# A second step's products moved into two accumulator banks, and the last accumulators copied in halves

## The chip, the cores and the metric

The kernel runs on one core of one Trainium2 chip. TensorE (PE) multiplies, VectorE (DVE) and ScalarE (ACT) do the elementwise work, SyncE (SP) issues most of the loads. The metric is the time of one execution on the device, in microseconds; the kernel before takes 663.96 (median of three runs, 663.55 to 664.05).

## The reference

Two small attentions exchange between 512 tokens and 32 states of each of 8 batches and 8 heads, and a two-layer network runs over the concatenated rows (8 x 544 = 4352 rows):

```python
scores = (x @ state.T) / 8;   a  = softmax(scores);   xread = a @ state      # 512 rows a batch
scores2 = (state @ x.T) / 8;  a2 = softmax(scores2);  sread = a2 @ x         # 32 rows a batch
y = concat(xread, sread)                    # (8 batches, 544 rows, 512 = heads x 64)
h = y @ w_in                                # 512 -> 2048
g = where(h >= 1, h, where(h <= -1, 0, (h + 1)**2 / 4))
out = g @ w_out                             # 2048 -> 512, all in float32
```

## The kernel before

`xread` is never formed: `state @ w_in` is computed instead ("states times W_in", `sw_product`, L410), and the attention's weights (`ath`, `atl`) are multiplied by it. Every float32 factor is split into a high and a low part of a shorter type, and a product is three matmuls: high by high, high by low, low by high (L477 to L479, L534 to L536).

A batch `b` goes through eight steps `j`; a step makes 256 of the 2048 hidden columns. In a step, `sw` of the step is made (sixteen small matmuls into the one `mm` tile, two banks), copied out as `swh` by ACT and `swl` by DVE; the *first products* (`Hidden.product`, L461) give two tiles of 128 hidden columns by 512 tokens, each from two halves `q` of the contraction and three matmuls a half, so twelve matmuls; ACT and DVE turn them into `g` (`relu`, `square`, `bound`, `high`, `low`, L481 to L502); and the *output products* (`g2`, L515) multiply `gh` and `gl` by the step's part of W_out into four accumulators of 128 tokens by 512, one bank each, with twenty-four matmuls that `g2` can issue in two halves. The four accumulators of a batch stay over its eight steps, and `store` (L542) copies them out in the last. The ninth "batch" is the 256 state rows of all batches together, with two accumulators and four steps; its `store` copies the first with ACT and the second with DVE, each followed by four DMAs of 32 rows.

PSUM has eight banks: two in the `mm` tile, two for the first products (`ps_h`, tag `h`), four with the tag `acc`. Ahead of the first output product the `acc` banks hold the score tiles of batch 0 (two) and `warmed`, into which filler matmuls go (`warm`, L195).

Batch 0 is special. Its weights are still on their way and have to be decoded: each chunk of W_in or W_out is loaded raw, ACT makes a high part (L588), ACT or DVE a low part (L580, L575), DVE joins them (L596), and for W_out ACT and DVE split the result (L603, L607). The order of this part is written by a planner (`Plan`, L23). Each operation is declared with an engine, a cost in microseconds, what it comes after, and which shared tile it takes. On PE and SP the order is that of the declarations; on ACT and DVE the planner simulates: whenever an engine is idle it starts the ready operation with the longest tail of costs behind it. Between the first scores and the first output product it puts fillers where it expects PE to idle (L125). After batch 0 the code is written in plain order (L807).

In that plan PE's declared order at the start is: scores, `sw0`, first half (`q` = 0) and second half of step 0's products, `sw1`, the transposes `e2p` of the second attention, step 1's products, `sw2`, first half of step 0's output products, `sr` (the second attention's read), second half, step 2's products, `sw3`, and so on (L776 to L789). A step's products take the two `h` banks once the `bound`s of the step before are through, and its buffer `u` once `gl` of the step before is.

Of the kernel before, what the change touches and what calls it, by code (L numbers as in the profile page):

```python
# [8 lines left out]
F32 = mybir.dt.float32  # L9
# [13 lines left out]
class Plan:  # L23
# [13 lines left out]
    def op(self, key, engine, cost, run, after=(), take=(), ends=()):  # L37

        after = list(after)
        prior = self.last.get(engine) if engine in ("PE", "SP") else None  # L40
        self.last[engine] = key
        self.ops[key] = [engine, cost, run, after, list(take), list(ends), prior]
# [95 lines left out]
def state_exchange_moe(  # L138
# [17 lines left out]
    nc = tc.nc  # L156
    B, P, NT, H, D = x.shape
    S = NT * P
    NS = 32
    DM = H * D  # L160
    NPR = H // 2
    CI = 256
    NC = w_in.shape[0]
# [3 lines left out]
    TOK = S + NS  # L167
# [5 lines left out]
    work = ctx.enter_context(tc.tile_pool(name="work", bufs=2))  # L173
# [4 lines left out]
    def ps_acc(name):  # L178
        return ps.tile([P, DM], F32, tag="acc", bufs=4, name=name)

    def ps_h(name):
        return ps.tile([P, 512], F32, tag="h", bufs=2, name=name)
# [6 lines left out]
    half = small.tile([P, 1], F32, name="half")  # L189
# [35 lines left out]
    class Attention:  # L225


        def __init__(self, b):
            self.b = b
            self.xt = loaded.pop(("xt", b))  # L230
            self.ath = work.tile([P, 2, S], F32R, tag="ath", name=f"ath{b}")
            self.atl = work.tile([P, 2, S], F32R, tag="atl", name=f"atl{b}")
            att_of[b] = (self.ath, self.atl)
# [196 lines left out]
    def sw_high(b, c):  # L430
        pt, wh, _ = sw_of[b, c]
        nc.scalar.copy(out=wh, in_=pt)

    def sw_low(b, c):
        pt, wh, wl = sw_of[b, c]
        nc.vector.tensor_tensor(out=wl, in0=pt, in1=wh.bitcast(F32), op=ALU.subtract)
# [14 lines left out]
    acc = {}  # L451

    class Hidden:


        def __init__(self, b, j):
            self.b, self.j = b, j
            self.u = work.tile([P, 2, S], F32, tag="u", bufs=1, name=f"u{b}_{j}")
            self.hs = []

        def product(self, i, ks=None):  # L461
            b, j = self.b, self.j
            n = n_of[b]
            per = S // n
            ah, al = att_of[b]
            nk = ah.shape[1]
            if not ks or 0 in ks:
                self.hs.append(ps_h(f"h{b}_{j}_{i}"))
            hp = self.hs[i]
            for r in range(per):  # L470
                f = (2 * j + i) * per + r
                wh, wl = chunk[b, f // 2]
                sl = slice((f % 2) * P, (f % 2 + 1) * P)
                o = hp[:, r * n:(r + 1) * n]
                for k in ks or range(nk):
                    first, last = k == 0, k == nk - 1
                    nc.tensor.matmul(o, lhsT=wh[:, k, sl], rhs=ah[:, k], start=first, stop=False)  # L477
                    nc.tensor.matmul(o, lhsT=wl[:, k, sl], rhs=ah[:, k], start=False, stop=False)  # L478
                    nc.tensor.matmul(o, lhsT=wh[:, k, sl], rhs=al[:, k], start=False, stop=last)  # L479
# [35 lines left out]
    def g2(b, j, half=None):  # L515
        n = n_of[b]
        per = S // n
        nt = n // P
        if b not in acc:
            acc[b] = [ps_acc(f"acc{b}_{t}") for t in range(nt)]  # L520
        gh, gl = gs[b, j]
        last = j == NJ // per - 1
        pairs = [(i, t) for i in range(2 * per) for t in range(nt)]
        if last:
            pairs.sort(key=lambda p: p[1])
        if half is not None:
            pairs = pairs[half * len(pairs) // 2:][:len(pairs) // 2]
        for i, t in pairs:
            f = 2 * per * j + i
            oh, ol = wo[f // 2][:, 0, f % 2], wo[f // 2][:, 1, f % 2]  # L530
            c0 = (i % per) * n + t * P
            lh, ll = (v[:, i // per, c0:c0 + P] for v in (gh, gl))
            a = acc[b][t]
            nc.tensor.matmul(a, lhsT=lh, rhs=oh, start=f == 0, stop=False)  # L534
            nc.tensor.matmul(a, lhsT=lh, rhs=ol, start=False, stop=False)  # L535
            nc.tensor.matmul(a, lhsT=ll, rhs=oh, start=False, stop=f == NF - 1)  # L536
            if last and i == 2 * per - 1:
                store(b, t)
# [3 lines left out]
    def store(b, t):  # L542
        if t == 0:
            outs[b] = rawp.tile([P, NT, DM], F32, tag="raw", name=f"o{b}")
        o = outs[b][:, t]
        if b == B and t % 2:
            nc.vector.tensor_copy(o, acc[b][t])
        else:
            nc.scalar.copy(out=o, in_=acc[b][t])  # L549
        if b < B:  # L550
            r0 = b * TOK + t * P
            nc.scalar.dma_start(out=out[r0:r0 + P, :], in_=o)
        else:
            for i in range(4):
                r0 = (4 * t + i) * TOK + S
                (nc.sync if i % 2 else nc.scalar).dma_start(
                    out=out[r0:r0 + NS, :], in_=o[i * NS:(i + 1) * NS]
                )

# [127 lines left out]
    def hidden_ops(b, j):  # L689
        k = (b, j)  # L690
        for i in range(2):
            op(("relu", i) + k, "ACT", 0.58, lambda i=i: hid[k].relu(i), [("p", i) + k], ends=[("h", i) + k],
               take=[("u", ("u",) + k)] if i == 0 else [])
        op(("square",) + k, "ACT", 0.97, lambda: hid[k].square(), [("relu", 0) + k, ("relu", 1) + k])
        for i in range(2):
            op(("bound", i) + k, "DVE", 0.6, lambda i=i: hid[k].bound(i), [("square",) + k], ends=[("h", i) + k])
        op(("gh",) + k, "ACT", 0.97, lambda: hid[k].high(), [("bound", 0) + k, ("bound", 1) + k],
           ends=[("u",) + k], take=[("g", ("g",) + k)])
        op(("gl",) + k, "DVE", 1.14, lambda: hid[k].low(), [("gh",) + k], ends=[("u",) + k])

    def tensor(key, cost, f, after=(), take=(), ends=()):
        op(key, "PE", cost, f, after, take, ends)
# [6 lines left out]
    def sw_ops(b, c, n):  # L709
        tensor(("sw", b, c), 0.35 + 0.35 * n, lambda: sw_product(b, c, n), [("w", c + i) for i in range(n)],  # L710
               take=[("mm", ("sw", b, c)), ("w", ("wc", b, c))])
        op(("swh", b, c), "ACT", 0.5 * n, lambda: sw_high(b, c), [("sw", b, c)], ends=[("sw", b, c)])
        op(("swl", b, c), "DVE", 0.6 * n, lambda: sw_low(b, c), [("swh", b, c)], ends=[("sw", b, c)])

    def g1_ops(b, j):
        if j == 0:
            for q in range(2):
                for i in range(2):
                    need = [(x, b, j) for x in ("swh", "swl")] + [(x, b, q) for x in ("ath", "atl")]
                    tensor(("p", i, b, j) if q else ("p0", i), 0.72, lambda i=i, q=q: product(i, b, j, [q]), need,  # L720
                           take=[] if q else [("h", ("h", i, b, j))], ends=[("wc", b, j)])
            return
        for i in range(2):
            need = [(x, b, j) for x in ("swh", "swl")] + [(x, b, q) for x in ("ath", "atl") for q in range(2)]
            tensor(("p", i, b, j), 1.4, lambda i=i: product(i, b, j), need, take=[("h", ("h", i, b, j))],
                   ends=[("wc", b, j)])

    def g2_ops(b, j, half):
        k = (b, j)
        tensor(("g2", half) + k, 2.75, lambda: g2(b, j, half), [("gh",) + k, ("gl",) + k, ("wol", j), ("sc done", 0)],  # L730
               ends=[("g",) + k])


# [21 lines left out]
    for side in range(2):  # L755
        tensor(("sc", 0, side), 0.6, lambda side=side: att_start(0, side), [("dma", "xt", 0, side)],
               ends=[("xt", 0)])
# [6 lines left out]
                          take=[("mm", ("e2p", 0))]),  # L764
        1: lambda: tensor(("sr", 0), 1.1, lambda: atts[0].read2(), [("kept", 0), ("dma", "xn", 0)],
                          take=[("mm", ("sr", 0))], ends=[("e2", 0), ("xn", 0)]),
        2: lambda: tensor(("sc", 1), 1.1, lambda: att_start(1), [("dma", "sb", 1), ("dma", "xt", 1)],
                          take=[("mm", ("sc", 1))], ends=[("xt", 1)]),
        3: lambda: tensor(("rt", 0), 0.3, lambda: atts[0].keep2(), [("rs", 0)], take=[("mm", ("rt", 0))]),
        4: lambda: tensor(("e2p", 1), 0.9, lambda: atts[1].turn2(), [("exp2", 1, 0), ("exp2", 1, 1)],  # L770
                          take=[("mm", ("e2p", 1))]),
        5: lambda: tensor(("sr", 1), 1.1, lambda: atts[1].read2(), [("kept", 1), ("dma", "xn", 1)],
                          take=[("mm", ("sr", 1))], ends=[("e2", 1), ("xn", 1)]),
        6: lambda: tensor(("rt", 1), 0.3, lambda: atts[1].keep2(), [("rs", 1)], take=[("mm", ("rt", 1))]),
    }
    for j in range(NJ):  # L776
        g1_ops(0, j)
        hidden_ops(0, j)
        if j + 1 < NC:
            sw_ops(0, j + 1, 1)  # L780
        if j:
            g2_ops(0, j - 1, 0)
        if j in between:
            between[j]()
        if j == 2:
            att_ops1(1)
            att_ops2(1)
        if j:
            g2_ops(0, j - 1, 1)  # L789
    sw_ops(1, 0, 2)  # L790
    import os
    with guard:
        plan.emit(warm, ("sc", 0, 0), ("g2", 0, 0, 0))

# [74 lines left out]
```

## Time and profile before

| | |
|---|---|
| median of three runs | 663.96 us (663.55 to 664.05) |
| the profiled execution's own time | 664.0 us |
| its span | 662.2 us |
| PE busy | 653.9 us (99%), 4442 matmuls |
| DVE busy | 340.3 us (51%) |
| ACT busy | 356.5 us (54%) |
| granted TensorE clock | 1.00 |
| HBM traffic | 34.08 MB read, 8.91 MB written |

The profile comes from one execution. A row of its timeline gives the start, the length, the engine, the line of the kernel and the tile written and read; "x12" merges neighbours. What stands in brackets is how long the engine was idle before the row and what ended that. Rows of one engine overlap by some 0.05 to 0.1 us, so that the distance of two starts is the better measure of an operation that runs back to back. A matmul's record (0.39 us) is longer than its distance from the next (0.23 us), because matmuls are pipelined.

### The profile page before, as it was taken

To read this page: it belongs to the slowest core of one execution; us is meant where nothing else is said; L and a number is where in the kernel's file an instruction comes from. 1 tells how busy PE (TensorE), PEld (TensorE's weight loads), DVE (VectorE), ACT (ScalarE), POOL (GpSimd) and SP (SyncE) were. 2 spreads that over 40 slices of the span, in tenths; PEclk is the share of its full clock that TensorE was granted. 3 is DMA by queue.
4 is the path that set the end of the run, shared out by engine and by line. 5 is a ranking of instruction groups with operands and counts; after the bars stand their busy time and mean duration, and the time that the engine had idled before them with its cause. 6 is when DMAs were issued, how large, how long until landed. Compare 5 with 4: busy or idle time off the path is not lost.

```text
span 662.2 us, 10304 instructions
## 1 busy us (share of the span) xinstructions
PE 653.9 (99%) x4442; PEld 514.2 (78%) x4442; DVE 340.3 (51%) x490; ACT 356.5 (54%) x462; POOL 0.8 (0%) x7
## 2 busy tenths in 40 slices
PE   8999999999999999999999999999999999999997
PEld 6677777777787777777787777777778777778896
DVE  5999947623673239433563338433563343333431
ACT  4899847544554446544554447444653454454642
POOL 0000000000000000000000000000000000000000
PEclk9999999999999999999999999999999999999999
DMA  8986103010301003010301002010100000000101
GB/s 359 400 359 249 64 10 119 0 65 0 120 10 64 1 4 124 0 65 0 128 1 64 1 24 105 0 65 0 65 1 1 1 33 32 1 1 1 63 1 33
DMA packets 11085, 43.65 MB, mean 66 GB/s; under 512 B 1312, under 2 KB 1440, under 8 KB 7968
## 3 DMA queue, kind: packets, MB, share of 16 engines
q1 hardware_dynamic: 6096, 34.28, 13.6%
q10 hardware_dynamic: 4944, 8.72, 3.5%
q8 instruction: 35, 0.57, 0.3%
q14 instruction: 10, 0.08, 0.0%
HBM read 34.08 MB, written 8.91 MB: 65 GB/s over the span
## 4 chain that ended last, share of the span: by engine, by line
PE 91%; ACT 5%; DVE 3%; issue 0%; DMA 0%; POOL 0%; SPq 0%; ACTq 0%; POOLq 0%
PE acc L534 19%; PE acc L536 18%; PE acc L535 18%; PE h L477 9%; PE h L479 9%; PE h L478 9%; PE sw L417 5%; PE sc L253 1%; PE sr L350 1%; PE e2p L333 1%; PE warmed L198 1%; ACT u L482 1%; ACT u L485 1%; ACT raw_i L588 1%; DVE w L596 1%; ACT wo L603 0%
## 5 line engine op out<-in xcount | busy, mean ns | idle before, releaser
L534 PE MATMUL acc<-wo,gh 128*128 128x512 f32 x544 | 218.8, 402 | 0.0
L535 PE MATMUL acc<-wo,gh 128*128 128x512 f32 x544 | 212.3, 390 | 0.0
L536 PE MATMUL acc<-wo,gl 128*128 128x512 f32 x544 | 212.2, 390 | 0.0
L482 ACT ACTIVATE u<-h,half 128x512 f32<-128x512 f32 x136 | 93.7, 693 | 219.9 <-PE h L479 202.6
L488 DVE SCALAR_TENSOR_TENSOR u<-u,h 128x512 f32<-128x512 f32 x136 | 87.0, 680 | 206.7 <-ACT u L485 206.7
L534 PEld LDWEIGHTS acc<-wo,gh 128*128 128x128 f32 x544 | 102.1, 188 | 40.1 <-ACT u L482 12.8
L536 PEld LDWEIGHTS acc<-wo,gl 128*128 128x128 f32 x544 | 102.1, 188 | 22.5 <-issue 0.4
L535 PEld LDWEIGHTS acc<-wo,gh 128*128 128x128 f32 x544 | 102.2, 188 | 19.4 <-DVE wo L607 0.3
L502 DVE TENSOR_TENSOR gl<-u,gh 128x1024 fp32r<-128x1024 f32 x68 | 83.2, 1224 | 33.0 <-ACT gh L497 32.0
L497 ACT CAST gh<-u 128x1024 fp32r<-128x1024 f32 x68 | 71.8, 1056 | 50.3 <-DVE u L488 49.9
L485 ACT ACTIVATE u<-u 128x1024 f32<-128x1024 f32 x68 | 72.5, 1065 | 1.3
L417 PE MATMUL sw<-w,sb 64*32 64x256 f32 x1024 | 36.0, 383 | 1.8 <-DVE w L596 1.3
L417 PEld LDWEIGHTS sw<-w,sb 64*32 64x32 f32 x1024 | 15.1, 106 | 17.9 <-issue 8.8
L479 PE MATMUL h<-atl,sw_0h 128*128 128x512 f32 x60 | 23.6, 393 | 0.3 <-DVE atl L306 0.2
L477 PE MATMUL h<-ath,sw_0h 128*128 128x512 f32 x60 | 23.5, 394 | 0.0
L549 ACT COPY o<-acc 128x512 f32<-128x512 f32 x33 | 18.6, 586 | 9.1 <-PE acc L536 9.0
L478 PE MATMUL h<-ath,sw_0l 128*128 128x512 f32 x60 | 23.5, 391 | 0.0
L479 PE MATMUL h<-atl,sw_6h 128*128 128x512 f32 x60 | 23.4, 389 | 0.0
L479 PE MATMUL h<-atl,sw_2h 128*128 128x512 f32 x60 | 23.4, 389 | 0.0
L477 PE MATMUL h<-ath,sw_2h 128*128 128x512 f32 x60 | 23.3, 389 | 0.0
L478 PE MATMUL h<-ath,sw_2l 128*128 128x512 f32 x60 | 23.3, 389 | 0.0
L477 PE MATMUL h<-ath,sw_4h 128*128 128x512 f32 x60 | 23.3, 389 | 0.0
(174 smaller groups left out, 735.0 us busy)
## 6 DMA issues: line engine op xcount, KB each, us to landing
xt<-in_xt_dram SPq DMA_DIRECT2D x16, 512.0 KB, 4.5
raw_i<-in_moe_w_in_dram SPq DMA_DIRECT2D x8, 1024.0 KB, 6.9
raw_o<-in_moe_w_out_dram SPq DMA_DIRECT2D x8, 1024.0 KB, 9.4
xn<-in_x_dram SPq DMA_DIRECT2D x8, 1024.0 KB, 6.4
out_dram<-o ACTq DMA_DIRECT2D x32, 256.0 KB, 2.0
sb<-in_state_dram SPq DMA_DIRECT2D x1, 448.0 KB, 12.6
out_dram<-o SPq DMA_DIRECT2D x4, 64.0 KB, 1.7
out_dram<-o ACTq DMA_DIRECT2D x4, 64.0 KB, 2.0
```

What stands on the lines that cost most here:

```text
L417: nc.tensor.matmul(pt[pr * NS:(pr + 1) * NS, hh, i * CI:(i + 1) * CI], lhsT=sb[rows, b, pr], rhs=w32[c + i][rows, pr], start=True, stop=True,)
L477: nc.tensor.matmul(o, lhsT=wh[:, k, sl], rhs=ah[:, k], start=first, stop=False)
L478: nc.tensor.matmul(o, lhsT=wl[:, k, sl], rhs=ah[:, k], start=False, stop=False)
L479: nc.tensor.matmul(o, lhsT=wh[:, k, sl], rhs=al[:, k], start=False, stop=last)
L482: nc.scalar.activation(out=self.u[:, i], in_=self.hs[i], func=AF.Relu, scale=0.5, bias=half)
L485: nc.scalar.activation(out=self.u, in_=self.u, func=AF.Square)
L488: nc.vector.scalar_tensor_tensor(out=self.u[:, i], in0=self.u[:, i], scalar=1.0, in1=self.hs[i], op0=ALU.min, op1=ALU.max,)
L497: nc.scalar.copy(out=gh, in_=self.u)
L502: nc.vector.tensor_tensor(out=gl, in0=self.u, in1=gh.bitcast(F32), op=ALU.subtract)
L534: nc.tensor.matmul(a, lhsT=lh, rhs=oh, start=f == 0, stop=False)
L535: nc.tensor.matmul(a, lhsT=lh, rhs=ol, start=False, stop=False)
L536: nc.tensor.matmul(a, lhsT=ll, rhs=oh, start=False, stop=f == NF - 1)
```

## The change

Three things are edited.

The second step of batch 0 (`(b, j) == (0, 1)`) takes two tiles of the `acc` tag for its products instead of two `h` banks, and the buffer of the tag `e2` for its `u`. Since these banks are two of the four accumulators that step 0's output products start to fill, these are now sorted by accumulator, and their second half waits for step 1's `bound`s.

In PE's declared order `sw1` goes between the first and the second half of step 0's products; `e2p` goes from in front of step 1's products to behind them; `sr` goes from between the halves of step 0's output products to behind both.

In the last `store`, ACT copies the left half of each accumulator and DVE the right one, and one DMA of 128 rows of 1 KB goes out on the ACT queue and one on the SP queue, instead of a whole copy by one engine and four DMAs of 32 rows of 2 KB, two on each queue.

```diff
         def __init__(self, b, j):
             self.b, self.j = b, j
-            self.u = work.tile([P, 2, S], F32, tag="u", bufs=1, name=f"u{b}_{j}")
+            tag = "e2" if self.early() else "u"
+            self.u = work.tile([P, 2, S], F32, tag=tag, bufs=1, name=f"u{b}_{j}")
             self.hs = []
+
+        def early(self):
+
+            return (self.b, self.j) == (0, 1)
...
-                self.hs.append(ps_h(f"h{b}_{j}_{i}"))
+                self.hs.append((ps_acc if self.early() else ps_h)(f"h{b}_{j}_{i}"))
...
-        if last:
+        if last or (b, j) == (0, 0):
             pairs.sort(key=lambda p: p[1])
...
-        if b == B and t % 2:
-            nc.vector.tensor_copy(o, acc[b][t])
-        else:
+        if b < B:
             nc.scalar.copy(out=o, in_=acc[b][t])
-        if b < B:
             r0 = b * TOK + t * P
             nc.scalar.dma_start(out=out[r0:r0 + P, :], in_=o)
         else:
-            for i in range(4):
-                r0 = (4 * t + i) * TOK + S
-                (nc.sync if i % 2 else nc.scalar).dma_start(
-                    out=out[r0:r0 + NS, :], in_=o[i * NS:(i + 1) * NS]
-                )
+            rows = out.rearrange("(b t) d -> b t d", b=B)[4 * t:4 * t + 4, S:S + NS]
+            lo, hi = slice(0, DM // 2), slice(DM // 2, DM)
+            nc.scalar.copy(out=o[:, lo], in_=acc[b][t][:, lo])
+            nc.vector.tensor_copy(o[:, hi], acc[b][t][:, hi])
+            nc.scalar.dma_start(out=rows[:, :, lo], in_=o[:, lo])
+            nc.sync.dma_start(out=rows[:, :, hi], in_=o[:, hi])
...
-               take=[("u", ("u",) + k)] if i == 0 else [])
+               take=[("e2" if k == (0, 1) else "u", ("u",) + k)] if i == 0 else [])
...
         if j == 0:
             for q in range(2):
+                if q:
+                    sw_ops(b, 1, 1)
                 for i in range(2):
...
-            tensor(("p", i, b, j), 1.4, lambda i=i: product(i, b, j), need, take=[("h", ("h", i, b, j))],
-                   ends=[("wc", b, j)])
+            tensor(("p", i, b, j), 1.4, lambda i=i: product(i, b, j), need,
+                   take=[("h", ("h", i, b, j))] if j > 1 else [], ends=[("wc", b, j)])
...
-        tensor(("g2", half) + k, 2.75, lambda: g2(b, j, half), [("gh",) + k, ("gl",) + k, ("wol", j), ("sc done", 0)],
+        need = [("gh",) + k, ("gl",) + k, ("wol", j), ("sc done", 0)]
+        if j == 0 and half == 1:
+            need += [("bound", i, 0, 1) for i in range(2)]
+        tensor(("g2", half) + k, 2.75, lambda: g2(b, j, half), need,
                ends=[("g",) + k])
...
         g1_ops(0, j)
         hidden_ops(0, j)
-        if j + 1 < NC:
+        if j == 1:
+            between[0]()
+        if 0 < j and j + 1 < NC:
             sw_ops(0, j + 1, 1)
         if j:
             g2_ops(0, j - 1, 0)
-        if j in between:
+        if j > 1 and j in between:
             between[j]()
         if j == 2:
             att_ops1(1)
             att_ops2(1)
         if j:
             g2_ops(0, j - 1, 1)
+        if j == 1:
+            between[1]()
```

## Rows read from the trace of the kernel before

**Rows 1.** Waits of PE, longest first: us in total, times, longest.
```profile
...
PE sw L417 <- ACT e L337: 0.5, 1, 0.5
...
```

**Rows 2.** Busy time by stretch: us, PE, PEld, DVE, ACT, POOL busy (count), clock, DMA, GB/s.
```profile
22.00:25.24 3.24, 2.75 (x28) 2.28 (x21) 2.92 (x7) 3.24 (x7) 0.00 (x0) 1.00 1.05 432
...
30.17:62.84 32.67, 32.51 (x249) 23.59 (x249) 31.05 (x40) 31.86 (x41) 0.00 (x0) 1.00 0.86 344
62.84:657.87 595.03, 595.03 (x3983) 470.89 (x3983) 286.12 (x407) 305.74 (x397) 0.00 (x0) 1.00 0.10 35
...
```

**Rows 3.** Timeline of PE, 22 to 37 us: start, length, what.
```profile
22.04 2.05 PE L198 MATMUL warmed<-ident 128*128 128x128 f32 x16
...
29.68 0.49 PE L534 MATMUL acc<-wo,gh 128*128 128x512 f32 x1
30.17 0.50 PE L535 MATMUL acc<-wo,gh 128*128 128x512 f32 x1
...
33.92 0.50 PE L534 MATMUL acc<-wo,gh 128*128 128x512 f32 x1
34.25 0.40 PE L535 MATMUL acc<-wo,gh 128*128 128x512 f32 x1
...
36.77 0.39 PE L477 MATMUL h<-ath,sw_2h 128*128 128x512 f32 x1
...
```

**Rows 4.** The chain that ended last, in order of time: start, us, what.
```profile
8.80 0.76 DVE z L260 x2
...
62.84 1.09 PE e2p L333 x8
...
```

**Rows 5.** Timeline of DVE, 18 to 33 us.
```profile
18.48 1.18 DVE L596 SCALAR_TENSOR_TENSOR w<-raw_i 128x1024 int32<-128x1024 int32 x1
...
25.75 0.69 DVE L575 TENSOR_SCALAR raw_o<-raw_o 128x1024 int32<-128x1024 uint32 x1
...
31.67 1.28 DVE L488 SCALAR_TENSOR_TENSOR u<-u,h 128x512 f32<-128x512 f32 x2 [0.27 <-ACT u L485]
...
```

**Rows 6.** Timeline of ACT, 18 to 34 us.
```profile
21.15 0.69 ACT L322 ACTIVATE e<-sc,nm 128x512 f32<-128x512 f32 x1 [1.94 <-DVE nm L319]
...
21.83 1.26 ACT L482 ACTIVATE u<-h,half 128x512 f32<-128x512 f32 x2
22.97 0.60 ACT L432 CAST sw_1h<-sw 128x512 fp32r<-128x512 f32 x1
23.43 1.08 ACT L485 ACTIVATE u<-u 128x1024 f32<-128x1024 f32 x1
...
27.99 1.04 ACT L337 COPY e<-e2p 128x1024 f32<-128x1024 f32 x1
...
31.47 1.18 ACT L588 ACTIVATE raw_o<-raw_o 128x1024 f32<-128x1024 f32 x1
...
```

**Rows 7.** Timeline of all engines, 48.9 to 50.9 us.
```profile
...
48.98 1.18 DVE L502 TENSOR_TENSOR gl<-u,gh 128x1024 fp32r<-128x1024 f32 x1
...
49.09 0.69 ACT L322 ACTIVATE e<-sc,nm 128x512 f32<-128x512 f32 x1 [0.78 <-DVE z L260]
...
50.52 0.50 PE L534 MATMUL acc<-wo,gh 128*128 128x512 f32 x1
...
```

**Rows 8.** Timeline behind the last matmul.
```profile
658.07 0.69 DVE L547 COPY o<-acc 128x512 f32<-128x512 f32 x1 [5.42 <-DMA out_dram<-o]
...
658.79 0.85 ACTq L556 DMA_DIRECT2D out_dram<-o  x2
```

**Rows 9.** ACT's groups by form: busy us, mean ns of one, idle before.
```profile
...
L549 ACT COPY o<-acc 128x512 f32<-128x512 f32 x33 | 18.6, 586 | 9.1 <-PE acc L536 9.0
...
L369 ACT COPY srT<-rt 128x128 f32<-128x128 f32 x8 | 2.1, 262 | 0.0
...
```

**Rows 10.** DMA issues of the page: count, KB each, median us from issue to landing.
```profile
...
out_dram<-o ACTq DMA_DIRECT2D x32, 256.0 KB, 2.0
...
out_dram<-o SPq DMA_DIRECT2D x4, 64.0 KB, 1.7
...
```

More of the change, by code (lines that the diff above doesn't have):

```diff
@@ L789, in state_exchange_moe @@
             g2_ops(0, j - 1, 1)
+        if j == 1:
+            between[1]()
     sw_ops(1, 0, 2)
-    import os
     with guard:
```

## Prediction

> **What bounds the kernel now.** I read the page's head first, then the waits of TensorE, then busy time by stretch, then the chain. The head, in the table above, shows PE 99% busy over the span. That share counts fillers: `warm` matmuls are PE work too. The waits [rows 1] are what tells: six in all, the four behind the first 15 us of 0.5 us or less, the longest of these for the copy of `e2p`, before the first output product; behind that the view names none. The stretches [rows 2] say the same: from 30.17 to 62.84 PE is busy for 32.51 of 32.67 us, and from there to 657.87, where its last matmul ends, without a hole, at a granted clock of 1.00 (the 2.4 GHz level). So a gain can come from two places only: the start, up to about 30 us, and the 4.33 us behind the last matmul.
>
> At the start the hole is plain in PE's own order [rows 3]. Behind the first step's products and `sw1` stand sixteen fillers, from 22.04 to 24.09, and the second step's products come only after `e2p`. But two facts speak against a large gain. First, between 22.00 and 25.24 ACT is busy 3.24 of 3.24 us and DVE 2.92 [rows 2]. Second, the chain that ended last [rows 4] runs on DVE and ACT from 8.80 on and comes to TensorE for good only at `e2p` of the next batch, at 62.84. PE's early work is not what the end waited for; the lists of ACT and DVE are.
>
> **The change part by part.** All sums are against the profiled execution: span 662.2, its time 664.0, so 1.8 us lie around the span. The median of the three runs, 663.96, is 0.04 lower, and I take that off at the end.
>
> *What moves on PE.* `sw1` goes in front of the second half of step 0's products; step 1's products follow these at once, in accumulator banks, since they no longer wait for the two `h` banks; `e2p` goes behind them and `sr` behind the second half of step 0's output products. No matmul is added or removed but fillers. So the same work stands before the first output product (L534 at 29.68, in earnest L535 at 30.17 once the low half of `wo0` is there) [rows 3], and the gain of the start is how much earlier that one can begin. It needs three things: `gh`/`gl` of step 0, both halves of `wo0`, and `sw2` finished ahead of it on PE, which needs the copy of `e2p` out of the one `mm` tile.
>
> *PE's side:* `sw1` needs the join at 18.48 [rows 5], done at 19.66, so it can run at about 19.7 to 20.3, before the second half of step 0's products. These may end up to its own 0.6 later, which costs nothing as long as ACT, whose ReLUs come behind an exp [rows 6], still has that exp to do. Step 1's products (12, some 2.85 as below) are then done at about 24.5 to 25.5. The fillers' time is won for PE, and that buys nothing by itself.
>
> *ACT's side* sets the start. From 21.15 to 29.03 ACT works without a pause [rows 6]: exp, two ReLUs, `sw_1h`, square, exp, one weight piece, `gh`, `wo`, and last the copy of `e2p` (27.99 + 1.04). Its start at 21.15 hangs on `nm` from DVE, which is fully occupied, and stays. What the change takes out of this row is `sw_1h`: it can run at 20.3 in the 1.94 us that ACT idles before 21.15. Inside the list it is worth 23.43 - 22.97 = 0.46 us. So the `e2p` copy ends at about 28.5, `sw2` runs to 29.15, the first output product starts there and the second one 0.34 later (the distance of 33.92 to 34.25) at 29.49 instead of 30.17: 0.68 us.
>
> *DVE's side* must keep up: from 21.05, when `nm` is done and ACT can start, it has `sw_1l`, the second `nm`, the join of `wo0`, a low part, two bounds, the join of `w2`, `gl` and the low part of `wo0`: without the 0.07 by which records overlap, and the sizes of [rows 5] (0.6 for 512 columns and the low parts, 1.13 for 1024, 1.2 for both bounds) that is 0.6 + 0.8 + 1.13 + 0.6 + 1.2 + 1.13 + 1.13 + 1.13 = 7.7, so 28.75 at best, 29.35 if the other low part (25.75 now) stays in between. Both fit 29.49. Upper bound of the start, if ACT's idle 1.94 were used better than I see: 30.17 - 28.75 = 1.4 us. Lower bound: nothing (the order of the planner costs 0.7 somewhere), or less, in the slow rival.
>
> *What is late next.* The second half of step 0's output products now waits for step 1's bounds, since its two accumulators are the banks of step 1's products. The first half runs from 29.15 to about 32.0 (12 products, as 33.92 to 36.77: 2.85). ACT: ReLU, ReLU, square behind the copy, now without `sw_2h` in between: 28.5 + 1.14 (21.83 to 22.97) + 1.08 (the square's own length) = 30.7 [rows 6], and DVE's bounds, 1.28 both [rows 5], to 32.0. It just fits, if ACT and DVE take these first; I count 0. `sr` comes two microseconds later than now and frees its tile at 36.0; the load into `xn` that waits for it stands on SP behind the weights of steps 3 and 4, which wait for joins, so I count nothing for it. PE would then stand 0.68 earlier at the products of step 2 (36.77 now) [rows 3].
>
> *Does it last?* PE has to find its inputs early, too. `gl` of step 2 ends at 50.16 for a product at 50.52 [rows 7], and at 62.84 there is no slack at all, since the chain passes there [rows 4]. With ACT and DVE only 0.46 ahead and PE 0.68 ahead, the slack of 0.36 shrinks to 0.14, and at 62.84 PE waits 0.22 more. What is left behind 62.84 is ACT's and DVE's own gain, 0.46. I take 0.5 for the start, between 0 and 1.4.
>
> *The last accumulators.* Now the last copy is one DVE instruction of 0.69 from 658.07, then four issues, two on each queue, of which ACT's second starts at about 659.2, halfway through its 0.85 [rows 8]. After it: ACT copies 256 columns, DVE 256, and each queue issues once. For 256 columns the page has nothing; between 128 (262 ns) and 512 (586 ns) on ACT [rows 9] a straight line gives 0.37 us, and DVE's lies between half of 0.69 and all of it; I take 0.42, near the half, as on ACT. May both read the bank at once? The nearest row is the second exp of a score tile: ACT idles 0.78 us before it until DVE's transpose, which reads the same columns, is over [rows 7]. So I count the two in series: 658.07 + 0.37 + 0.06 + 0.42 = 658.92, issue at 658.95, against 659.2 now: 0.25. The transfers have 128 rows of 1 KB instead of 32 of 2 KB; the 128-row stores of the other batches land 2.0 us after their issue, the 32-row ones on SP 1.7 [rows 10]. Between -0.1 (the longer landing, no gain in waits) and 0.7 (both copies at once, issue at 658.5) I take 0.2, near the series.
>
> The Trainium skill bears on this: PSUM — Partial Sum Buffer, "PSUM bank collisions raise a hardware error", says that two engines must never touch the same bank and quadrant in one cycle, reads against reads and disjoint columns included. By that rule the halves, two sets of columns of one bank, must never overlap, and the tail's copies are the series of 0.25 with no parallel case at all; the turn-taking in the trace is over the same columns, so no run here shows disjoint ones yet.
>
> **Sum:** 0.5 + 0.2 = 0.7; 664.0 - 0.7 - 0.04 = 663.3 us.
>
> **The rivals.**
> *A, larger:* the planner packs ACT's idle 1.94 us better, the start gains 1.1 and the tail 0.4 (copies in part side by side, fewer final waits): 662.5. For it: 3 us of fillers vanish. Against it: DVE's list of 7.7 us leaves 1.4 at the very most, and all of it must survive 62.84.
> *B, nothing at the start:* the gate is ACT and DVE, whose order changes while their work doesn't; PE only waits in other places (at `sw2`, at 50.5, at 62.84). Tail alone: 663.75. For it speaks the chain [rows 4]; against it `sw_1h`, which does leave the list.
> *C, slower:* the new wait decides. If ACT takes two weight pieces of 1.18 like the one at 31.47 ahead of step 1's ReLUs, and DVE a join of 1.13 ahead of the bounds, these end at 32.0 + 2.36 + 1.13 = 35.5, PE stands 3.5 us in the middle of step 0's output products, and the time is 663.96 - 0.88 + 3.5 = 666.6. It decides from bounds later than 32.0, and makes the kernel measurably slower from about 34.3 on. Against it: these pieces serve step 1's output products, which are due later.
> *D, the tail as drawn does not come:* copies in series and longer landings cancel: 663.5 with the start's 0.5.
>
> **Numbers.** 0.2% is 1.33 us, and what a measurement can tell. The forecast 45% (its own range 662.7 to 663.8), A 20%, B 17%, C 6%, D 12%. Faster than 662.63 takes most of A and a little of the forecast: 0.19. Slower than 665.29 is C: 0.05. The rest, 0.76, is within. The range leaves out the outer half of A's bound and C: 662.1 to 664.4.
>
> **What would show it.** Right: `sw_1h` near 20.3 on ACT and absent from the list behind 21.15; fillers of 22 to 24 gone; L535's first at 29.3 to 29.7; the wait at `e2p` of batch 1 grown; half copies one after the other, one issue on each queue near 658.9 less the start's gain. Wrong: first output product before 28.9 (A) or after 30 (B); a wait of the output products for DVE's `u` at L488 of 2 us or more (C); DVE's half copy starting together with ACT's. A wait of PE anywhere behind 64 us would mean that I missed a slack.

## The result, and the profile after

The changed kernel takes 666.31 us (665.65 to 667.57, median of six) against 663.75 (662.98 to 664.05) for the kernel before on the same chip: ratio 1.0044, 95% interval 1.0032 to 1.0056. It is slower by 2.6 us; 663.3 was forecast, and the range ended at 664.4.

The profiled execution took 667.05 us, with a span of 665.3 instead of 662.2. TensorE's last matmul now ends at 658.65 instead of 657.87 [rows 2]: 0.78 us were lost before it, by these two executions as they stand. From there to the end it is 665.3 - 658.65 = 6.65 us instead of 4.33: 2.32 us were lost behind it. The two add up to the 3.1 of the span, and they have nothing to do with each other.

The two executions did not begin alike, though. These are DVE's second operations on the first scores, ahead of all that the change moves, before and after:

```profile
8.78 0.78 DVE L260 STREAM_TRANSPOSE z<-sc 128x256 f32<-128x256 f32 x2 [0.16 <-PE sc L253]
```

```profile
7.88 0.78 DVE L260 STREAM_TRANSPOSE z<-sc 128x256 f32<-128x256 f32 x2 [0.17 <-PE sc L253]
```

The changed kernel's execution is 0.90 us ahead here, and not by the change: in the six runs below that keep the start of before, this row lies between 7.85 and 8.79, and with the changed start of e1 it is at 8.60. Counted from this row, the last matmul is 0.78 + 0.90 = 1.68 us late. "Counted" below means this; times without the word are as the profiles have them.

**Behind the last matmul.** The timeline of the changed kernel, DVE, ACT and the two queues (the answer to [rows 8]):

```profile
656.53 0.42 DVE L559 COPY o<-acc 128x256 f32<-128x256 f32 x1 [3.12 <-ACT o L558]
659.25 0.42 DVE L559 COPY o<-acc 128x256 f32<-128x256 f32 x1 [2.29 <-ACT o L558]
...
658.84 0.37 ACT L558 COPY o<-acc 128x256 f32<-128x256 f32 x1 [2.35 <-PE acc L541]
659.24 0.55 ACTq L560 DMA_DIRECT2D out_dram<-o  x1
...
656.98 3.26 SPq L561 DMA_DIRECT2D out_dram<-o  x2
```

The copies are as forecast, 0.37 and 0.42 us, one after the other, and DVE's released by ACT's. What follows is not: from DVE's last copy (659.67) to the end of the span pass 5.6 us. The DMA view of 655 to 668 us shows why. First the kernel before (a row not shown so far), then the changed one; 40 slices of 0.325 us, busy share of the 16 DMA engines in tenths, and GB/s:

```profile
DMA  0000039980000079930000000000000000000000
GB/s 0 0 0 0 0 88 214 271 227 6 0 0 0 0 183 214 315 95 0 0 0 0 0 25 0 0 0 0 0 0 0 0 0 0 0 0 0 0 0 0
DMA packets 385, 0.53 MB, mean 41 GB/s; under 512 B 128, under 2 KB 128, under 8 KB 384
```

```profile
DMA  0000000002222222222222222220000000000000
GB/s 0 0 0 0 0 0 0 0 16 25 57 95 101 95 95 101 95 95 101 88 101 88 85 98 98 91 79 13 0 0 0 0 0 0 25 0 0 0 0 0
DMA packets 529, 0.53 MB, mean 41 GB/s; under 512 B 16, under 2 KB 528, under 8 KB 528
```

The same 0.53 MB leave before in two short bursts, four slices each, at up to 315 GB/s with nearly all engines busy; after, in one long plateau near 95 GB/s with a share of 2 tenths. The stretches give that share more exactly (columns as in [rows 2]):

```profile
658.65:660.50 1.85, 0.15 (x1) 0.00 (x0) 0.42 (x1) 0.37 (x1) 0.00 (x0) 1.00 0.27 97
660.50:662.50 2.00, 0.00 (x0) 0.00 (x0) 0.00 (x0) 0.00 (x0) 0.00 (x0) 1.00 0.27 94
```

0.27 of 16 is 4.3, about four engines. The packets under 512 B tell the same: read as the marks of the landings, they are 128 before for eight DMAs, so 16 each, and 16 after for four DMAs, so 4 each. The new source and target of a store are `[4, 32, 256]`: four batches outside. The Trainium skill has this rule, in DMA: Bandwidth & Descriptors, "Rules for kernel authors" ("Use all 16 engines"): an outermost dimension smaller than 16 confines a DMA to at most that many engines. The trace agrees: a share of 0.27, and 4 marks a DMA instead of 16. The prediction didn't use that rule, which spoke against this change.

**Up to the last matmul.** TensorE's waits behind the first 20 us (the answer to [rows 1]), and the stretches of the start ([rows 2]):

```profile
PE sw L417 <- ACT e L337: 1.1, 1, 1.1
PE rt L364 <- DVE sw_4l L436: 0.7, 1, 0.7
PE acc L541 <- DVE gl L507: 0.5, 1, 0.5
PE acc L539 <- ACT gh L502: 0.3, 1, 0.3
```

```profile
25.24:28.89 3.65, 2.08 (x25) 0.97 (x23) 3.55 (x7) 3.65 (x7) 0.00 (x0) 1.00 1.01 426
28.89:32.30 3.41, 3.09 (x7) 2.48 (x8) 3.41 (x6) 3.41 (x5) 0.00 (x0) 0.50 1.02 430
32.30:63.10 30.80, 30.09 (x239) 21.68 (x238) 28.55 (x36) 28.55 (x36) 0.00 (x0) 1.00 0.82 325
```

Two things stand there. In 25.24 to 28.89 PE is busy for 2.08 of 3.65 us only, and in the 3.41 us after it the granted clock is 0.50, the 1.2 GHz level. And where [rows 2] had no hole, in the thirty microseconds behind, PE now stands 0.71 us: the wait of `rt` for `sw_4l`. The timeline of PE shows the fall (the answer to [rows 3]):

```profile
27.95 0.50 PE L539 MATMUL acc<-wo,gh 128*128 128x512 f32 x1 [0.28 <-ACT gh L502]
28.29 0.39 PE L540 MATMUL acc<-wo,gh 128*128 128x512 f32 x1
29.21 0.79 PE L541 MATMUL acc<-wo,gl 128*128 128x512 f32 x1 [0.53 <-DVE gl L507]
29.80 0.63 PE L539 MATMUL acc<-wo,gh 128*128 128x512 f32 x1
...
31.93 0.57 PE L541 MATMUL acc<-wo,gl 128*128 128x512 f32 x1
32.34 0.39 PE L539 MATMUL acc<-wo,gh 128*128 128x512 f32 x1
...
36.91 0.50 PE L482 MATMUL h<-ath,sw_2h 128*128 128x512 f32 x1
```

The first output product starts 1.73 us earlier than before (27.95 against 29.68), which is 0.83 counted. But from 29.21 to 32.34 there are only seven matmuls, 0.45 apart instead of 0.23: 3.13 - 7 x 0.23 = 1.5 us lost. Step 2's products start at 36.91, not earlier than before (36.77), and 1.04 later counted.

### The profile page after: what moved, and what is told of

Read it like the earlier page. It is cut to its first block, busy times and chain, and to the rows that moved or that the text cites. A ratio compares the mean times of both kernels' runs of the same rounds, so it can differ in the third digit from the quotient of the medians.

```text
span 665.3 us, 10289 instructions
## 1 busy us (share of the span) xinstructions
PE 653.2 (98%) x4436; PEld 514.4 (77%) x4436; DVE 340.7 (51%) x491; ACT 356.6 (54%) x463; POOL 0.8 (0%) x7
## 4 chain that ended last, share of the span: by engine, by line
PE 93%; ACT 3%; DVE 2%; issue 1%; POOL 0%; POOLq 0%
PE acc L539 20%; PE acc L541 18%; PE acc L540 18%; PE h L482 10%; PE h L483 9%; PE h L484 9%; PE sw L417 5%; PE sr L350 1%; PE sc L253 1%; PE e2p L333 1%; PE warmed L198 1%; ACT u L487 0%; ACT wo L606 0%; ACT e L322 0%; DVE w L599 0%
## 5 line engine op out<-in xcount | busy, mean ns | idle before, releaser
L483 PE MATMUL h<-ath,sw_4l 128*128 128x512 f32 x60 | 23.4, 389 | 0.0
```

## The experiments

Four questions: which half of the change costs, why the stores are slow, when the clock falls, and where the start's gain goes. All were timed beside the kernel before (663.43 for e1 to e4, 663.38 for e5 to e8, 663.80 for e9 to e11).

**e1: the change without its store.**

```diff
+        if b == B and t % 2:
+            nc.vector.tensor_copy(o, acc[b][t])
+        else:
+            nc.scalar.copy(out=o, in_=acc[b][t])
...
+            for i in range(4):
+                r0 = (4 * t + i) * TOK + S
+                (nc.sync if i % 2 else nc.scalar).dma_start(
+                    out=out[r0:r0 + NS, :], in_=o[i * NS:(i + 1) * NS]
+                )
```

> The changed kernel with the last store of before (whole copies, four DMAs of 32 rows of 2 KB). Theory: most of the loss is the new store, whose four DMAs each use only 4 of the 16 DMA engines and run one after the other, 1.55 us each, 2.3 us in all; without it 666.31 - 2.3 = 664.0 us, and the stretch behind PE's last matmul is 4.3 us again, not 6.65. Rival: the loss is the start (PE at half clock from 28.9 to 32.3 us, and the wait at 53.7), and the store costs at most 0.5: 665.8.

663.78 (663.37 to 665.39), ratio 1.0008 (0.9999 to 1.0017). Most of the loss is gone with the store, and the profile has 4.33 us behind the last matmul again. But the start gives no gain. In the profiled execution the clock stayed up, though PE pauses as in the changed kernel:

```profile
25.24:28.89 3.65, 2.40 (x31) 1.68 (x29) 3.62 (x8) 3.65 (x5) 0.00 (x0) 1.00 1.00 422
28.89:32.30 3.41, 2.88 (x13) 2.10 (x12) 3.41 (x6) 3.41 (x5) 0.00 (x0) 1.00 1.03 435
```

Counted, this execution is 0.95 us ahead of before at the first output product (28.55), 0.57 at step 2's products (36.02), and 0.28 behind at the last matmul. In between it waits at `rt`:

```profile
PE rt L364 <- DVE sw_4l L436: 0.9, 1, 0.9
```

**e2: the kernel before with the new store alone.**

> The kernel before with only the last store of the change. Theory: 663.75 + 2.3 = 666.05 us, with 4 landing marks per DMA instead of 16 and a stretch of about 6.6 us behind the last matmul. Rival (the start is to blame): at most 664.2.

665.54 (665.05 to 666.03), ratio 1.0029 (1.0017 to 1.0041): 2.1 us for the store by itself. Its DMA view (655 to 668 us) shows the plateau again, on a start that is that of before:

```profile
DMA  0000112222222222222222100000010000000000
```

The 2.11 of the store and the 0.35 of the rest (e1) are 2.46 of the 2.56 of the whole, which is the same within the intervals.

**e3: half copies, but the four DMAs of 32 rows of 2 KB.** In the kernel before:

```diff
+            nc.scalar.copy(out=o[:, lo], in_=acc[b][t][:, lo])
+            nc.vector.tensor_copy(o[:, hi], acc[b][t][:, hi])
             for i in range(4):
...
```

> The kernel before with the copies in halves (ACT left, DVE right), but the four DMAs of 32 rows of 2 KB behind both. It tells the copies from the DMAs. Theory: the halves run in series, 0.37 + 0.03 + 0.42 = 0.82 against 0.69, so +0.13: 663.9 us. Rival: the halves are what costs, 2 us or more: 666.

663.72 (663.32 to 664.12), ratio 1.0003 (0.9994 to 1.0012). The copies in halves neither cost nor gain what can be told.

**e4: half copies, eight DMAs of 32 rows of 1 KB an accumulator.**

```diff
+                nc.scalar.dma_start(out=out[r0:r0 + NS, lo], in_=o[i * NS:(i + 1) * NS, lo])
+                nc.sync.dma_start(out=out[r0:r0 + NS, hi], in_=o[i * NS:(i + 1) * NS, hi])
```

> The kernel before with the copies in halves and eight DMAs of 32 rows of 1 KB for each accumulator, the left halves on the ACT queue and the right ones on SP: rows of 1 KB, but each DMA over the 16 engines. Theory (the split over 4 engines costs): four issues of 0.4 a queue instead of two, +0.8, and the copies' 0.1: 664.6 us, with transfers that overlap. Rival (rows of 1 KB are slow by themselves): 666 or more.

664.62 (664.13 to 665.01), ratio 1.0018 (1.0009 to 1.0027): 1.2 us. Rows of 1 KB over all engines are dearer than the old store, but cheaper than four engines. The issues are longer: ACT's for the last accumulator take 1.74 us instead of 0.85 [rows 8], and SP's, which begin only behind DVE's half, end last (SP's row spans both accumulators):

```profile
658.08 1.74 ACTq L556 DMA_DIRECT2D out_dram<-o  x4
```

```profile
655.81 4.45 SPq L557 DMA_DIRECT2D out_dram<-o  x8
```

So the last issue of all ends at 660.26 instead of 659.64 [rows 8], though the last matmul starts 0.39 earlier (657.25 against 657.64): 1.0 us, most of the loss.

**e5: whole copies, one DMA of 4 x 32 rows of 2 KB an accumulator.**

```diff
+            rows = out.rearrange("(b t) d -> b t d", b=B)[4 * t:4 * t + 4, S:S + NS]
+            (nc.sync if t % 2 else nc.scalar).dma_start(out=rows, in_=o)
```

> The kernel before with whole copies by one engine as before, but one DMA for each of the last two accumulators, over the four batches' row blocks (4 x 32 rows of 2 KB) in place of four DMAs of 32 rows. It tells the number of engines from the size of the rows and from the halves. Theory: such a DMA has 4 landing marks and uses 4 engines, 32 rows of 2 KB on each at about 0.085 us or more, so 2.7 us and more where the four DMAs overlap in 1.1: about +1.5 us, 664.9. Rival (rows of 1 KB or halves are what costs): one issue fewer, 663.1.

668.31 (668.21 to 668.78), ratio 1.0073 (1.006 to 1.0087): 4.9 us. The rows of 2 KB and the copies are those of before, so neither the row's length nor the copies are needed for the loss. A single large DMA on one queue is not the cause either: the stores of the other batches are such DMAs of 256 KB, with 128 rows outside, and land 2.0 us after their issue [rows 10]. What is left is the shape, four outside. Its DMA view, 655 to 668 us:

```profile
DMA  0000000412212122222232112222211000000000
GB/s 0 0 0 0 0 0 19 44 6 13 13 25 63 69 113 95 101 107 101 88 25 13 44 57 82 88 101 101 101 63 44 25 13 0 0 0 0 0 0 0
```

The direction is what the four engines ask for, the size is over three times the expected one. The second DMA is issued only at 658.73, behind the last copy, and by the rates its bytes follow those of the first (they dip to 13 GB/s at 662 us, with 0.29 MB before and 0.24 behind). Both begin at a low rate (6 to 69 GB/s for some 2.6 us, then 13 to 88 for some 1.6) before they reach the plateau near 100. Why they begin so slowly was not settled.

**e6: e1 with fillers.** Eight calls of `warm` ahead of `sw2` and four ahead of the first output product:

```diff
-                if begun[first] < begun[k] < begun[until]:
+                if begun[first] < begun[k] <= begun[until]:
+                    n = {("sw", 0, 2): 8, until: 4}.get(k, n)
```

> The changed kernel with the last store of before, and more fillers on TensorE where it waited in the start: 8 in place of 4 in front of sw2, 4 new ones in front of the first output product. Theory (idle TensorE loses its clock in some executions and that makes the slow ones among the runs of the same kernel without fillers, 665.1 and 665.4): no execution with a clock under 0.999, and none over 664.3; the median as without, 663.8. Rival (the clock has nothing to do with the waits at the start): the same spread.

663.85 (663.58 to 664.28), ratio 1.0006 (0.9998 to 1.0015). The median is that of e1, the spread is not: e1 has two executions above 665 (665.07 and 665.39, with mean granted clocks of 0.997 and 0.996), e6 none above 664.28 at 0.999 to 1.000. Two of eleven against none show little by themselves; e7, e8 and e11 below bear it out. Busy time in e6, in the stretches used above:

```profile
25.24:28.89 3.65, 3.57 (x43) 2.97 (x41) 3.62 (x7) 3.65 (x6) 0.00 (x0) 1.00 1.01 429
28.89:32.30 3.41, 3.41 (x16) 2.52 (x15) 3.41 (x6) 3.41 (x5) 0.00 (x0) 1.00 1.01 421
```

**e7: e1 with `rt`, which waited 0.9 us there, put behind the second half of step 2's output products. e8: e7 with the fillers of e6.**

```diff
-        if j > 1 and j in between:
+        if j > 1 and j != 3 and j in between:
             between[j]()
...
-        if j == 1:
-            between[1]()
+        if j in (1, 3):
+            between[j]()
```

> The changed kernel with the last store of before, and the transpose rt of batch 0 behind the second half of step 2's output products, not between the halves, where TensorE waits 0.9 us for sw_4l. Theory (the start gains 0.75 us and this wait takes it back): 662.9 us, 0.5 below before. Rival (some other wait of the same size appears as soon as this one goes, since the lists of ACT and DVE set the end): 663.6 to 663.9.

665.03 (663.62 to 665.73), ratio 1.0022 (1.0013 to 1.0030): the theory that `rt` was the last obstacle fell. The profiled execution is one in which the clock fell, in the same stretch as in the changed kernel:

```profile
28.89:32.30 3.41, 2.88 (x8) 2.19 (x8) 3.41 (x6) 3.41 (x5) 0.00 (x0) 0.63 1.02 430
```

> Both of the last two edits, with the last store of before. Theory: 662.8 us and no execution with a lowered clock at the start. Rival: 663.6 or more.

663.85 (663.58 to 664.53), ratio 1.0007 (0.9998 to 1.0015). In e7, six of the eleven executions have a mean clock of 0.996 or 0.997, and spans of 663.2 to 663.9; the other five have 661.8 to 662.8. In e8 none is below 0.998. A mean clock has to be read with care, since the clock also falls behind the last matmul: in e8's profile it is 0.50 from 660 us to the end and 1.00 in all of the start, which gives 0.998, and the longer end of e2 gives 0.997. Among kernels with the old store, 0.996 and 0.997 with a longer span are taken here for a fall at the start; e7's profile, at 0.997, shows one. So the fall of the clock costs some 1.1 us where it comes in e7, and the fillers keep it away: without them it came in eight of 22 executions (e1 and e7, which are alike up to step 2's output products), with them in none of 22 (e6 and e8). But where the clock stays up, the kernel still is not faster than before: the wait at `rt` is gone, and its place is taken by one of 1.2 us at `e2p` of the next batch, for `sw_5l`. The waits of PE in e8 behind 20 us, and the timeline of its DVE:

```profile
PE e2p L334 <- DVE sw_5l L437: 1.2, 1, 1.2
```

```profile
59.73 1.22 DVE L602 SCALAR_TENSOR_TENSOR wf<-raw_o 128x1024 int32<-128x1024 int32 x1
60.87 1.22 DVE L602 SCALAR_TENSOR_TENSOR w<-raw_i 128x1024 int32<-128x1024 int32 x1
62.00 0.68 DVE L437 TENSOR_TENSOR sw_5l<-sw,sw_5h 128x512 fp32r<-128x512 f32 x1
```

In DVE's list `sw_5l` stands at 62.00 here and at 62.10 before, but e8's execution began much earlier. The fair comparison is e2, which has the start of before and whose execution began about as early (the row on the scores at 7.85, here 7.68; in both the chain then waits for the first chunk of W_out, which lands at 14.9): against it PE is 0.57 us ahead at step 2's products (35.59 against 36.16), and `sw_5l` is 0.55 late (62.00 against 61.45). DVE is not starved there, it makes a join first that is due later.

**e9: e8 with `sw_5h` ahead of a weight piece on ACT and `sw_5l` ahead of that join on DVE.** The planner's order is kept but for two operations, the weight piece and the join, each put further back:

```diff
+MOVED = [(("high", "o", 6), ("square", 0, 4)), (("w", 7), ("bound", 0, 0, 4))]
...
+        for k, ahead in MOVED:
+            order.remove(k)
+            order.insert(order.index(ahead), k)
```

> The kernel with the old store, the fillers and rt late, in which PE waited 1.17 us at e2p of the next batch (62.74) for DVE's sw_5l. Here ACT makes sw_5h ahead of a weight piece (1.16) and DVE makes sw_5l ahead of a join (1.22); no work is added or removed. Theory 1 (the time won at the start, 0.75 us at step 2's products, is still there at 61.4, and is lost only because that one low part stands behind a join): e2p starts at 61.6 to 61.8, nothing else becomes late since ACT waits for PE most of the time behind 63, and the time is 0.7 to 1.0 below the kernel before, 662.4 to 662.7. Theory 2 (ACT's and DVE's lists are full, so that what is put behind becomes the next thing late): e2p comes early, but PE waits as long for another result between 62 and 80, and the time stays at 663.4 to 663.9.

663.05 (662.68 to 663.37) against 663.80, ratio 0.9991 (0.9982 to 1.0000). `sw_5l` is made at 60.70, `e2p` starts at 61.44, and PE no longer stands anywhere from 32 to 63 us. Against e2 again, `e2p` is 0.75 earlier (62.19 there); the 1.40 against the profile of before is in part that execution's late beginning. The time lies between the two forecasts.

```profile
60.70 0.69 DVE L442 TENSOR_TENSOR sw_5l<-sw,sw_5h 128x512 fp32r<-128x512 f32 x1
61.30 1.23 DVE L607 SCALAR_TENSOR_TENSOR w<-raw_i 128x1024 int32<-128x1024 int32 x1
```

```profile
32.30:63.10 30.80, 30.79 (x247) 22.40 (x246) 29.52 (x38) 29.45 (x37) 0.00 (x0) 1.00 0.82 326
```

**e10: the control, `sw_5l` ahead of a low part in the kernel before.**

```diff
+MOVED = [(("low", "i", 7), ("bound", 0, 0, 4))]
```

> The control: the kernel before, with sw_5l put ahead of one low part (0.69) on DVE, so that it ends at about 62.1 instead of 62.7. Theory 1 (in the kernel before PE itself is the limit up to 62.84: it stands only about 0.3 us there): a gain of 0 to 0.3, 663.1 to 663.4. Rival (DVE's list alone sets the start, in the kernel before as well): the whole 0.6, 662.8.

663.27 (662.75 to 663.68), ratio 0.9995 (0.9986 to 1.0004). Counted, `e2p` starts 0.33 earlier than before here. Most of what e9 gains may be had without the change: a point estimate of 0.5 here against 0.75 there, each uncertain by about 0.6, and the 0.5 lies between the two forecasts. That e9 beats e10 is not shown; that it beats the kernel before is at the edge of the interval.

**e11: the kernel before without the fillers ahead of `e2p`.**

```diff
-                    n = int((begun[k] - idle) / 0.34)
+                    n = 0 if k == ("e2p", 0) else int((begun[k] - idle) / 0.34)
```

> The kernel before without the sixteen filler matmuls ahead of e2p, so that PE idles some 2.0 us more between 22 and 24.4; nothing else changes. Theory 1 (a PE that pauses in 22 to 29 can have its clock halved some us later, which is what costs the changed kernel about 1.5 us in the executions where it happens): the profile or some of the runs show a stretch at granted clock 0.5 of about 3.4 us, those runs are 1.3 to 1.7 us longer, others like the kernel before; median 663.4 to 665, with a spread of over 1.5 us. Rival (fillers do nothing): 663.4, spread as before.

664.39 (663.60 to 664.71), ratio 1.0011 (1.0002 to 1.0020). Eight of its eleven executions have a mean clock of 0.996 or 0.997, with spans of 662.2 to 662.9 but for one of 662.0; the three others have 1.000 and spans of 661.8 to 662.0; the kernel before has none below 0.999 in 27. The profiled execution is one of the three, so no row shows the stretch itself, and the loss is smaller than expected: a median 0.6 us above the kernel before, and a spread of 1.1 instead of over 1.5. A pause at the start is dear on this kernel, and the sixteen fillers of [rows 3] were not idle time.

## Why the prediction was wrong

**The step that failed is the tail's.** "Between -0.1 (the longer landing, no gain in waits) and 0.7 (both copies at once, issue at 658.5) I take 0.2." The measured value is -2.1 (e2) to -2.3 (the two profiles). Everything up to the issue was right: 0.37 and 0.42, in series, DVE's copy through at 659.67, which is the forecast 658.92 and the 0.78 by which the last matmul came later. What was mis-sized is the landing: it was priced at 0.3 at most (2.0 against 1.7), and four engines in place of sixteen cost over 2. I took it from the 128-row stores of the other batches, 2.0 us [rows 10], as if 128 rows were the likeness that counts; those have 128 rows outside, these have four. The lower bound was too narrow by a mechanism, not by a size: none of the rows that the prediction reads shows a store with four outside, so the landing was unknown, and four engines instead of sixteen should have been a rival. That rival C's 666.6 lies near the measured 666.31 is chance: the wait from which C has it did not come.

**The term of the start, 0.5, failed too: it was -0.35 in e1 (interval -1.1 to 0.1, so no gain that can be told), and -1.68 counted in the profiled execution, where the clock fell.** By its steps:
- `sw_1h` out of the list: right (19.35, or 20.25 with the 0.90 by which this execution began early; forecast 20.3). The first output product came 0.3 earlier than forecast (27.95 + 0.90 = 28.85 against 29.15), and at step 2's products e1 is 0.57 ahead, near the forecast 0.68.
- "What is late next", the bounds of step 1: right, they ran at 30.29 to 31.56 and nobody waited; rival C did not occur.
- Fillers at nothing ("the fillers' time is won for PE, and that buys nothing by itself"): wrong in sign. Eight records are left (24.86), PE then waits 1.09, 0.28 and 0.53 us, and in some executions the clock falls; e7, e8 and e11 show that this follows the fillers.
- "What is left behind 62.84 is ACT's and DVE's own gain, 0.46": wrong, and this is the step that failed where the clock stays up: e1 is 0.34 behind, counted, at `e2p` of the next batch. What leaves ACT's list does not leave DVE's, and the planner orders both anew: in the changed kernel it puts a low part on ACT and a join on DVE in front of `sw_4`, so that `sw_4l` is made at 53.70 (53.03 in e1) instead of 52.35, and in e8 a join in front of `sw_5l`. That is rival B's picture, "PE only waits in other places", though with the wait at `rt`, which it did not name. e9 against e8 (0.9991 and 1.0007 of the kernel before, some 1.1 us) shows that this order is what held e8 back. That anything of the start's own gain is then kept is not shown, since the same swap alone gives e10 its 0.5.

The sum of the start in the profiled execution, counted: 0.8 earlier at the first output product, 1.5 lost to the clock, some 0.3 more than before to `gl`, and 0.7 at `rt`: 1.7 late, as the last matmul is.

## What to carry to other kernels

A store that merges several DMAs into one is to be judged by the outermost dimension of its pattern, not by its bytes or its rows: with four outside it ran on four engines here, 95 GB/s against up to 315. Where a planner writes the order, an operation taken out of one engine's list is a gain only if the results that the bound engine needs next are still made first; look at the last wait and swap that one. Before two profiles are compared by absolute times, compare a row that stands ahead of all that was changed: here it lay 0.90 us apart. And fillers that keep TensorE busy ahead of a run of matmuls may belong to the cost of the run: whoever takes them away looks at the granted clock behind them.

## What the runs showed of the hardware that was not expected

- A store of 128 rows with an outer dimension of four: share 0.27 of 16 engines, 94 to 97 GB/s, and one after the other for four such stores on two queues.
- In the changed kernel the clock fell to the 1.2 GHz level at 28.89 us, although PE's longest pause in the 14 us before it was 1.09 us (2.08 us busy of the last 3.65). It falls only in some executions of the same kernel: by the mean clocks in six of eleven in e7, eight of eleven in e11, two of eleven in e1, none in e6 and e8.
- Half a bank costs more than half, as the prediction's straight line had it: 0.37 us for 256 columns on ACT against 0.59 for 512 [rows 9], 0.42 against 0.69 on DVE [rows 8].
